# The first phase of an attention and two-layer feed-forward kernel put in order by a list scheduler in the kernel's source

## The chip, the cores and the metric

The kernel runs on one core of one Trainium2 chip. The metric is device time in microseconds (us), lower is better, taken from whole runs; beside them stands one profiled execution, from which every row below comes. The engines are TensorE (PE; its weight loads are listed as PEld), VectorE (DVE), ScalarE (ACT), GpSimd (POOL) and SyncE (SP), which issues the transfers. Each works through its own instructions in the order in which the program lists them.

## What is computed

Causal local attention with a few global keys, then two feed-forward layers:

```python
scores = scale * np.matmul(q, k.transpose(0, 1, 3, 2))      # 4 batches, 8 heads, 768 tokens, 64 wide
keep = is_global | is_local                                  # first 8 keys, or the last 96
scores = np.where(keep, scores + bias, -1e9)                 # bias: minus slope[head] * distance
a = softmax(scores)
x = (a @ v)          # as 3072 tokens x 512
h = x @ w_in         # 512 -> 2048
x = (h - np.tanh(h)) @ w_out
h = x @ w_in2
out = (h * np.cos(h)) @ w_out2
```

The weights of both layers arrive as 8-byte floats.

## The kernel before

**Split numbers.** Each operand of a large product is held as a high part, rounded to the engine's 4-byte format, and a low part, which is the rest. A product is three matmuls: high by high, high by low, low by high. So every value that goes into a matmul costs a copy (high) and a subtraction (low) on some engine.

**Phases.** Phase 0 is the attention and, woven into it, the first half (chunks 0 to 7, of 128 hidden units each) of layer one. Phase 1 is the other half of layer one, phases 2 and 3 are layer two. Only phase 0 is reordered by the change.

**Attention.** A tile i is 128 tokens (24 of them); a quad is a tile and one of two groups g of four heads (48 of them, numbered n = 2i + g). A quad passes these steps: load q and k (`load_qk`); transpose them on PE (`qk_T`, L301 and L303); form high parts on ACT (`qk_hi`, L311, L312) and low parts on DVE (`qk_lo`, L318, L320, L323, L326); scores on PE (`att_s`, L342, 12 matmuls); bias and row minimum on DVE (`att_e`, L362, four a quad); exponent on ACT (L365, four); the sum's reciprocal on DVE (L373, L374) and the four products with it on DVE (`att_n`, L378); transposes on PE (`att_t`, L388, two groups of four, two in the first tile of a batch) copied out by ACT (L390, tile `pt`); and the product with v on PE (`att_v`, L404). After both quads of a tile `att_x` forms the high part of x on ACT (L419) and the low part on DVE (L420), in the tile `xt`.

**Feed-forward of phase 0.** A block j is 256 tokens, which are tiles 2j and 2j + 1; there are 12. For each of its eight chunks f, `ffn_in` runs 12 matmuls (L456), takes tanh on ACT (L464), subtracts on DVE (L465), copies the high part on DVE (L470) and forms the low part on POOL (L471); `ffn_out` runs 12 matmuls (L486) two chunks later. IN(j) below is the first L456 matmul of block j: it needs the low part of tile 2j + 1.

**Weights.** A half is 128 rows or columns of a weight, 512 KB as loaded; phase 0 uses 16. Each passes scale and tail on ACT (L68, L76), join on DVE (L85 and L88), split, which is the high part, on ACT (L97), and the low part on POOL (L98). The 16 halves of phase 1 pass the same steps during phase 0.

**Order.** `in_order` holds each engine to the order in which the source writes phase 0: five `early_quad` calls, then one `quad` call for each further quad, which interleaves attention steps, four `ffn_step` calls (one `ffn_in` or `ffn_out` each) and weight steps (`w_stage`) by hand. `busy` issues matmuls on zeros (L694) where PE would stand idle early on.

Of the kernel before, what the change touches and what calls it, by code (L numbers as in the profile page):

```python
# [102 lines left out]
def attention_ffn_kernel(ctx, tc, q, k, v, n_global, n_local, w1_in, w1_out, w2_in, w2_out, out):  # L103
# [249 lines left out]
    def att_e(i, g, z, pool=None):  # L353

        s, sm, n, m0 = Sb[i, g]
        if pool is None:
            e = pa.tile([128, 2, 256], F32, tag="e", name="e", bufs=3)
        else:
            e = pool.tile([128, 2, 256], F32, tag=("wi", "wo")[z], name="e", bufs=16)
        for j in range(2):  # L360
            col = i * H + 4 * g + 2 * z + j
            nc.vector.tensor_tensor_reduce(  # L362
                out=e[:, j, 0:n], in0=s[j][:, z, 0:n], in1=M[:, z, m0:m0 + n], scale=slopes[4 * g + j] / base,
                scalar=BIG, op0=ALU.add, op1=ALU.min, accum_out=nmall[:, col:col + 1])
            nc.scalar.activation(  # L365
                out=e[:, j, 0:n], in_=e[:, j, 0:n], func=AF.Exp, scale=-1.0,
                bias=nmall[:, col:col + 1], accum_out=sm[:, 2 * z + j:2 * z + j + 1])
        Eb[i, g, z] = e
# [576 lines left out]
```

## Time and profile before

| | us |
|---|---|
| median of three runs (1295.86 to 1297.28) | 1297.21 |
| the profiled execution | 1296.1 |
| its span, first to last instruction | 1294.3 |
| PE, DVE, ACT, POOL busy in the span | 1258.1, 777.7, 571.9, 387.0 |

PE is busy for 97% of the span. A busy share says little by itself where PE waits inside a stretch for other engines: the rows below cut the span where blocks of phase 0 begin. The profiled execution's own time lies 1.1 us under the median of the runs, and 1.8 us over its span.

### The profile page before, as it was taken

The page shows a single profiled execution, that of the slowest core. Times are in us where ns is not written, and L with a number is a line of the kernel's source. Part 1 is how long each engine was busy: PE and PEld are TensorE (multiplying, and loading weights), DVE is VectorE, ACT ScalarE, POOL GpSimd, SP SyncE. Part 2 cuts the span into 40 slices and gives each one's busy share as a digit, 9 for nine tenths or more (in the row PEclk, how much of TensorE's full clock was granted, in tenths as well). Part 3 has the DMA queues.
Part 4 walks back from the last instruction along what each step waited for, and adds up shares of the span by engine and source line. Part 5 has one row for each costly group of instructions (what it writes and reads, how often), then busy time and mean ns, then how long its engine had stood idle before and what let it go on. Part 6 is the DMA issues. An engine that isn't in the chain of part 4 may idle for free.

```text
span 1294.3 us, 20600 instructions
## 1 busy us (share of the span) xinstructions
PE 1258.1 (97%) x7627; PEld 1073.5 (83%) x7630; DVE 777.7 (60%) x1813; ACT 571.9 (44%) x1287; POOL 387.0 (30%) x343
## 2 busy tenths in 40 slices
PE   7779999999999999999999999999999999999997
PEld 4669999999989998888888888888888888888886
DVE  6986677676667642443443456777765565555563
ACT  6865556656556631322332334454444333323331
POOL 1441222222222232544543542333332222222221
PEclk9989999999999999999999999999999999999999
DMA  9424444433343461634554333323220322332110
GB/s 279 139 60 111 113 120 117 125 101 106 97 124 103 111 212 49 211 105 144 197 189 130 131 130 109 122 79 130 82 93 37 130 66 90 106 122 74 65 66 36
DMA packets 160845, 149.28 MB, mean 115 GB/s; under 512 B 84960, under 2 KB 119776, under 8 KB 160736
## 3 DMA queue, kind: packets, MB, share of 16 engines
q1 hardware_dynamic: 160448, 147.88, 36.2%
q8 instruction: 62, 1.02, 0.3%
q14 instruction: 47, 0.39, 0.1%
q10 hardware_dynamic: 288, 0.00, 0.0%
HBM read 103.81 MB, written 44.04 MB: 114 GB/s over the span
## 4 chain that ended last, share of the span: by engine, by line
PE 87%; DVE 6%; ACT 5%; issue 1%; DMA 1%; SPq 0%; DVEq 0%; ACTq 0%
PE h L456 39%; PE o L490 20%; PE o L486 10%; PE c L486 8%; PE x L404 3%; PE s L342 3%; ACT e L365 2%; PE tp L388 2%; DVE wf L85 1%; PE tp L301 1%; DVE e L362 1%; DVE wf L88 1%; DVE e L378 1%; ACT pt L390 1%; PE tp L303 1%
## 5 line engine op out<-in xcount | busy, mean ns | idle before, releaser
L471 POOL TENSOR_TENSOR g<-t,g 128x512 fp32r<-128x512 f32 (+1 forms) x240 | 263.9, 1100 | 767.0 <-DVE g L470 677.8
L456 PE MATMUL h<-x,wi 128*128 128x512 f32 x1728 | 423.4, 394 | 0.0
L456 PEld LDWEIGHTS h<-x,wi 128*128 128x128 f32 x1728 | 324.1, 188 | 75.9
L490 PE MATMUL o<-wo,g 128*128 128x512 f32 x1152 | 275.5, 390 | 0.0
L490 PEld LDWEIGHTS o<-wo,g 128*128 128x128 f32 x1152 | 216.2, 188 | 47.1
L465 DVE TENSOR_TENSOR t<-h,t 128x256 f32<-128x256 f32 (+1 forms) x144 | 73.5, 511 | 212.1 <-ACT t L464 211.9
L456 PE MATMUL h<-xt,wi 128*128 128x256 f32 x1152 | 165.2, 294 | 2.7 <-DVE xt L420 2.6
L486 PE MATMUL c<-g,wo 128*128 128x256 f32 x1152 | 161.4, 290 | 0.0
L456 PEld LDWEIGHTS h<-xt,wi 128*128 128x128 f32 x1152 | 147.2, 195 | 9.0 <-issue 4.1
L464 ACT ACTIVATE t<-h 128x256 f32<-128x256 f32 (+1 forms) x144 | 65.0, 452 | 202.9 <-PE h L456 198.6
L486 PEld LDWEIGHTS c<-g,wo 128*128 128x128 f32 x1152 | 145.0, 192 | 2.1 <-issue 1.9
L441 ACT ACTIVATE t<-t 128x512 f32<-128x512 f32 x96 | 60.8, 633 | 192.4 <-DVE t L440 192.2
L365 ACT ACTIVATE e<-e,nmall 128x256 f32<-128x256 f32 (+1 forms) x192 | 92.8, 485 | 107.5 <-DVE nmall L362 107.5
L486 PE MATMUL o<-g,wo 128*128 128x512 f32 x576 | 139.1, 390 | 0.0
L486 PEld LDWEIGHTS o<-g,wo 128*128 128x128 f32 x576 | 108.1, 188 | 23.8
L443 DVE SCALAR_TENSOR_TENSOR t<-t,h 128x512 f32<-128x512 f32 x96 | 65.9, 686 | 102.0 <-ACT t L442 101.8
L470 DVE CAST g<-t 128x512 fp32r<-128x512 f32 (+1 forms) x240 | 95.2, 397 | 26.4 <-DMA yd<-g 5.2
L438 DVE SCALAR_TENSOR_TENSOR t<-ki,h 128x512 f32<-128x512 int32 x96 | 65.8, 685 | 67.6 <-ACT ki L437 67.2
L437 ACT ACTIVATE ki<-h 128x512 int32<-128x512 f32 x96 | 57.1, 598 | 107.9 <-PE h L456 107.6
L439 DVE SCALAR_TENSOR_TENSOR t<-ki,t 128x512 f32<-128x512 int32 x96 | 87.2, 908 | 2.8
L388 PE MATMUL tp<-ident,e 128*128 128x128 f32 x352 | 57.0, 282 | 15.6 <-ACT pt L390 13.9
L362 DVE CUSTOM_DVE_ANT_0 e<-s,M 128x256 f32<-128x256 f32 (+1 forms) x192 | 68.4, 397 | 4.5 <-PE s L342 3.9
(83 smaller groups left out, 1169.0 us busy)
## 6 DMA issues: line engine op xcount, KB each, us to landing
x<-yd SPq DMA_DIRECT2D x48, 512.0 KB, 5.5
raw<-in_moe_w_in_dram SPq DMA_DIRECT2D x26, 512.0 KB, 3.9
xd<-xt SPq DMA_DIRECT2D x12, 1024.0 KB, 5.4
raw<-in_moe_w_out_dram SPq DMA_DIRECT2D x24, 512.0 KB, 3.5
x<-xd SPq DMA_DIRECT2D x24, 512.0 KB, 6.8
yd<-g SPq DMA_DIRECT2D x24, 512.0 KB, 4.1
qn<-in_q_dram SPq DMA_DIRECT2D x48, 128.0 KB, 2.7
kn<-in_k_dram SPq DMA_DIRECT2D x48, 128.0 KB, 3.2
```

The lines of the kernel that those rows point to most:

```text
L362: nc.vector.tensor_tensor_reduce(out=e[:, j, 0:n], in0=s[j][:, z, 0:n], in1=M[:, z, m0:m0 + n], scale=slopes[4 * g + j] / base, scalar=BIG ...
L365: nc.scalar.activation(out=e[:, j, 0:n], in_=e[:, j, 0:n], func=AF.Exp, scale=-1.0, bias=nmall[:, col:col + 1], accum_out=sm[:, 2 * z + j: ...
L388: nc.tensor.transpose(tp[:, 2 * c + j], e[:, j, c * 128:(c + 1) * 128], ident)
L438: mark[1] = nc.vector.scalar_tensor_tensor(out=r, in0=ki, scalar=-C1, in1=h, op0=ALU.mult, op1=ALU.add)
L439: nc.vector.scalar_tensor_tensor(out=r, in0=ki, scalar=-C2, in1=r, op0=ALU.mult, op1=ALU.add)
L443: nc.vector.scalar_tensor_tensor(out=r, in0=r, scalar=-0.5, in1=h, op0=ALU.add, op1=ALU.mult)
L456: nc.tensor.matmul(h, lhsT=wk[:, a], rhs=x[:, b], start=(n == 0), stop=(n == 3 * KC - 1))
L465: mark[1] = nc.vector.tensor_tensor(out=t, in0=h, in1=t, op=ALU.subtract)
L470: nc.vector.tensor_copy(out=g[:, 0], in_=t)
L471: nc.gpsimd.tensor_tensor(out=g[:, 1], in0=t, in1=g[:, 0].bitcast(F32), op=ALU.subtract)
L486: nc.tensor.matmul(o[z], lhsT=w[:, a, z * 128:(z + 1) * 128], rhs=g[:, b], start=(f == 0 and n == 0 and (P > 0 or z % 2 == 0)), stop=(last ...
L490: nc.tensor.matmul(o[z], lhsT=g[:, a, z * 128:(z + 1) * 128], rhs=w[:, b], start=(f == 0 and n == 0), stop=(last and n == 2))
```

## The change

The hand-written calls of phase 0 are replaced by `Plan`, a list scheduler that runs while the kernel is built. Each step is an `op` with an engine, a cost and a latency in us, a rank, the steps that it needs, and the buffers that it takes and gives back. `solve` repeatedly starts, on the engine that can start first, the op of lowest rank among those that could start within 0.12 us of the earliest; the resulting order is written out and held by `in_order`. `ffn_in` and `ffn_out` are split into their single steps for this, with matmuls in groups of six. The work of phases 1 to 3 is as before.

Beside the order, some steps move between engines in phase 0. The low part of the 16 weight halves of phase 0 goes from POOL to DVE (those of phase 1 stay on POOL). The high part of g goes from DVE (L470) to ACT. In tiles 2 to 7 half of the products with the reciprocal (z = 1) go from DVE to ACT. `fill` puts matmuls on zeros where the plan sees PE idle in its first 100 us: there are 92 of them instead of 45, 22 at the start instead of 5. The last 11 steps of phase 0's feed-forward stay outside the plan. Chunks per block are eight, as before.

```diff
+class Plan:
...
+    def solve(self, near=0.12, look=60, fill=None, switch=0.09):
...
+                first = min(t for t, o in can)
+                t, o = min(((t, o) for t, o in can if t <= first + near), key=lambda c: (c[1]["rank"], c[0]))
+                if best is None or t < best[0]:
+                    best = t, o
...
+    def low(self, w, a, engine):
+        engine.tensor_tensor(out=w[:, 1], in0=a.bitcast(F32), in1=w[:, 0].bitcast(F32), op=ALU.subtract)
...
+    on_act = [(i, 1) for i in range(2, 8)]
...
+            if (i, z) in on_act:
+                nc.scalar.activation(out=e[:, j, 0:n], in_=e[:, j, 0:n], func=AF.Copy, scale=sm[:, c:c + 1])
...
+        if P == 0:
+            nc.scalar.activation(out=g[:, 0], in_=Gt[P, j, f], func=AF.Copy)
+        else:
+            nc.vector.tensor_copy(out=g[:, 0], in_=Gt[P, j, f])
...
+    plan = Plan(s=1, h=2, tp=1, x=1, c0=1, c1=1, e=3, pt=3, q2=2, sm=3, qk=0, v=3, xt=2, g=3, t=3, raw=RAWS, wf=2)
...
+            plan.op(("load",) + key, "SP", 1.6, -11 + 0.6 * m if m < n0 else r - 4, w_load_far if far else w_load,
...
+            plan.op(("low",) + key, *(("DVE", 0.62) if m < n0 else ("POOL", 1.4)), r - 1.4,
+                    lambda key=key, m=m: sp.low(W[key], part.pop(key), nc.vector if m < n0 else nc.gpsimd),
...
+    plan_loads()
+    plan_attention()
+    rest = 11
...
+    plan_weights(plan_ffn(steps), n0, n1)
+    for o in plan.solve(fill=fill):
+        o["run"]()
...
-    for n in range(5):
-        early_quad(n)
-    for n in range(5, len(quads) + 2):
-        if n == 12:
-            flag_n()
-        quad(n)
```

In the changed kernel the lines that answer to those above are: transposes L385 and L387, scores L426, L446 for L362, L454 for L365, products L469 (ACT) and L471 (DVE), transposes of e L481, copy L487, v L501, x L513 and L518, IN L561, tanh L570, subtraction L575, high part of g L583 (ACT), low part of g L590, OUT L615, join L156 and L159, weight low part L171, zeros L825.

**SP, the first transfers.** q and k of tile 0 come first (four rows), then, before the change:

```order
L283 DMA qn_121<-in_q_dram 128x4x64
L283 DMA kn_123<-in_k_dram 128x4x64
L290 DMA vn_125<-in_v_dram 128x8x64
L59 DMA raw_127<-in_moe_w_in_dram 128x4x256
L283 DMA qn_129<-in_q_dram 128x4x64
L283 DMA kn_131<-in_k_dram 128x4x64
```

and after it:

```order
L374 DMA vn_144<-in_v_dram 128x8x64
L130 DMA raw_146<-in_moe_w_in_dram 128x4x256
L130 DMA raw_148<-in_moe_w_in_dram 128x4x256
L367 DMA qn_197<-in_q_dram 128x4x64
L367 DMA kn_199<-in_k_dram 128x4x64
L130 DMA raww_201<-in_moe_w_in_dram 128x4x256
L374 DMA vn_208<-in_v_dram 128x8x64
L130 DMA raww_229<-in_moe_w_out_dram 128x1024
L367 DMA qn_257<-in_q_dram 128x4x64
L367 DMA kn_259<-in_k_dram 128x4x64
```

The last pair in each is q and k of tile 1, second group: three more weight halves and one more v stand ahead of it than before; 12 further halves follow it before anything else.

**DVE, the work around the low part of x of tile 1** (xt), before the change:

```order
L378 TENSOR_SCALAR e<-e,sm 128x256 x4
L85 SCALAR_TENSOR_TENSOR wf<-raww 128x512
L88 SCALAR_TENSOR_TENSOR wf<-raww,wf 128x512
L318 SCALAR_TENSOR_TENSOR q_548<-tp,qs,q_548 128x256
L320 TENSOR_TENSOR kw_96<-tp,kw_96 128x2x128
L326 CAST kw_96<-kg_98 128x4x32
L373 TENSOR_SCALAR sm<-sm 128x4
L374 RECIPROCAL sm<-sm 128x4
L378 TENSOR_SCALAR e<-e,sm 128x256 x4
L420 TENSOR_TENSOR xt<-x,xt 128x4x128
```

and after it:

```order
L471 TENSOR_SCALAR e<-e,sm 128x256 x4
L171 TENSOR_TENSOR wi<-wf,wi 128x512 x2
L156 SCALAR_TENSOR_TENSOR wf<-raww 128x512
L159 SCALAR_TENSOR_TENSOR wf<-raww,wf 128x512
L156 SCALAR_TENSOR_TENSOR wf<-raww 128x512
L159 SCALAR_TENSOR_TENSOR wf<-raww,wf 128x512
L171 TENSOR_TENSOR wo<-wf,wo 128x512
L156 SCALAR_TENSOR_TENSOR wf<-raww 128x512
L159 SCALAR_TENSOR_TENSOR wf<-raww,wf 128x512
L171 TENSOR_TENSOR wi<-wf,wi 128x512
L518 TENSOR_TENSOR xt<-x,xt 128x4x128
```

Joins and the new low parts of weights (L171) now fill DVE here, and the attention of later quads has moved behind.

**PE, where a later block begins** (the last row is its IN), before the change:

```order
L342 MATMUL s<-kw_97,q_4883 128x256 x12
L404 MATMUL x<-pt,vn 64x128 x8
L486 MATMUL c_4686<-g,wo 128x256 x6
L486 MATMUL c_4687<-g,wo 128x256 x6
L388 MATMUL tp<-ident,e 128x128 x2
L456 MATMUL h<-xt,wi 128x256 x12
```

and after it:

```order
L615 MATMUL c_4724<-g,wo 128x256 x6
L481 MATMUL tp<-ident,e 128x128 x2
L615 MATMUL c_4725<-g,wo 128x256 x6
L426 MATMUL s<-kw_97,q_4974 128x256 x12
L501 MATMUL x<-pt,vn 64x128 x8
L481 MATMUL tp<-ident,e 128x128 x2
L426 MATMUL s<-kw_96,q_5106 128x256 x12
L561 MATMUL h<-xt,wi 128x256 x24
```

The x row is the product with v that completes the block's input. Between it and IN stood 12 OUT matmuls and two transposes; now two (elsewhere four) transposes and the 12 score matmuls of the next quad, and all OUT matmuls of the old block come earlier.

## Rows read from the trace of the kernel before

**Rows 1.** Windows; columns: stretch, length, busy PE, PEld, DVE, ACT, POOL, clock, DMA share, GB/s.

```profile
0.00:40.90 40.90, 32.71 (x218) 19.89 (x221) 29.50 (x116) 27.84 (x80) 7.11 (x18) 1.00 1.01 283
40.90:94.70 53.80, 41.22 (x341) 38.05 (x341) 48.46 (x111) 38.61 (x94) 23.43 (x20) 0.90 0.26 72
94.70:135.60 40.90, 38.23 (x352) 36.07 (x351) 25.54 (x95) 20.89 (x60) 6.56 (x9) 0.96 0.35 95
135.60:465.70 330.10, 325.46 (x3061) 306.45 (x3060) 225.01 (x786) 198.75 (x566) 74.45 (x89) 1.00 0.40 110
```

**Rows 2.** Timeline of PE: start, length, instruction, idle time before; blocks 0 to 2 begin.

```profile
1.20 2.31 PE L694 MATMUL idle<-zero 128*128 128x512 bf16 x5 [1.20 <-DVE zero L699]
...
40.91 0.38 PE L456 MATMUL h<-xt,wi 128*128 128x256 f32 x1
...
94.66 0.36 PE L456 MATMUL h<-xt,wi 128*128 128x256 f32 x1
...
135.61 1.68 PE L456 MATMUL h<-xt,wi 128*128 128x256 f32 x12
```

**Rows 3.** Waits, 41 to 135 us: total, times, longest.

```profile
PE tp L388 <- ACT pt L390: 11.3, 5, 4.8
```

**Rows 4.** Lines, 41 to 94.7 us, of DVE and POOL: busy, mean ns, idle before.

```profile
L88 DVE SCALAR_TENSOR_TENSOR wf<-raww,wf 128x512 int32<-128x512 int32 x12 | 11.6, 970 | 0.4
L85 DVE SCALAR_TENSOR_TENSOR wf<-raww 128x512 int32<-128x512 int32 x12 | 10.8, 901 | 0.0
L378 DVE TENSOR_SCALAR e<-e,sm 128x256 f32<-128x256 f32 x16 | 7.4, 520 | 0.1
...
L98 POOL TENSOR_TENSOR wo<-wf,wo 128x512 fp32r<-128x512 f32 x7 | 9.8, 1401 | 5.4 <-ACT wo L97 5.4
L98 POOL TENSOR_TENSOR wi<-wf,wi 128x512 fp32r<-128x512 f32 x5 | 8.2, 1642 | 2.6 <-ACT wi L97 2.6
L471 POOL TENSOR_TENSOR g<-t,g 128x256 fp32r<-128x256 f32 x8 | 6.3, 784 | 23.2 <-DVE g L470 17.6 <-DVE sm L373 5.7
```

**Rows 5.** Timeline of DVE early on, and 60 us later beside POOL.

```profile
19.82 0.69 DVE L85 SCALAR_TENSOR_TENSOR wf<-raw 128x512 int32<-128x512 int32 x1
...
21.22 0.48 DVE L318 SCALAR_TENSOR_TENSOR q<-tp,qs,q 128x256 fp32r<-128x256 f32 x1
...
21.96 0.41 DVE L362 CUSTOM_DVE_ANT_0 e<-s,M 128x256 f32<-128x256 f32 x1
...
22.30 0.42 DVE L362 CUSTOM_DVE_ANT_0 e<-s,M 128x256 f32<-128x256 f32 x1
...
28.66 1.14 DVE L378 TENSOR_SCALAR e<-e,sm 128x256 f32<-128x256 f32 x4
...
32.20 0.69 DVE L420 TENSOR_TENSOR xt<-x,xt 128x512 fp32r<-128x512 f32 x1
...
62.09 1.84 POOL L98 TENSOR_TENSOR wi<-wf,wi 128x512 fp32r<-128x512 f32 x1 [0.85 <-ACT wi L97]
...
62.81 1.67 DVE L88 SCALAR_TENSOR_TENSOR wf<-raww,wf 128x512 int32<-128x512 int32 x1
```

**Rows 6.** DMA view, 0 to 41 us.

```profile
DMA packets 18292, 11.59 MB, mean 283 GB/s; under 512 B 13168, under 2 KB 17264, under 8 KB 18288
```

**Rows 7.** DMA issues of the whole span: KB each, median us to landing.

```profile
qn<-in_q_dram SPq DMA_DIRECT2D x48, 128.0 KB, 2.7
```

**Rows 8.** Timeline of all engines where block 5 begins.

```profile
243.43 0.98 PE L342 MATMUL s<-kw,q 64*128 64x256 f32 x12
...
244.34 1.09 PE L404 MATMUL x<-pt,vn 128*64 128x128 f32 x16
...
245.48 0.60 ACT L419 ACTIVATE xt<-x 128x512 fp32r<-128x512 f32 x1 [2.10 <-PE x L404]
246.11 0.69 DVE L420 TENSOR_TENSOR xt<-x,xt 128x512 fp32r<-128x512 f32 x1 [2.40 <-ACT xt L419]
...
247.04 0.36 PE L456 MATMUL h<-xt,wi 128*128 128x256 f32 x1
```

More of the change, by code (lines that the diff above doesn't have):

```diff
@@ L27 @@
 RAWS = 2
+RAMP = 16
 @contextmanager
@@ L351, in attention_ffn_kernel, with att_r @@
     Eb = {}
-    def att_e(i, g, z, pool=None):
+    def att_r(i, g, z, j, pool=None):
         s, sm, n, m0 = Sb[i, g]
[L356 to L368, printed above, removed]
@@ L478, in ffn_out @@
+        ffn_cast(P, j, f)
+        ffn_low(P, j, f)
+    def ffn_out(P, j, f, zs=range(4)):
+        w, g = W[P // 2, f, "wo"], G[P, j, f]
+        first, last = (f == chunks(P, j)[z] for z in (0, -1))
+        if first and P == 0 and zs[0] == 0:
             c = [ps_c.tile([128, 2, N1], F32, tag=f"c{z}", name=f"c{z}", bufs=1) for z in range(2)]
             acc[P, j] = [c[z // 2][:, z % 2] for z in range(KC)] + c
-        elif f == 0:
+        elif first and P > 0:
             acc[P, j] = [late["ps_o"][z // 2].tile([128, 512], F32, tag=f"o{z}", name=f"o{z}", bufs=1) for z in range(4)]
@@ L482, in ffn_out @@
         o = acc[P, j]
-        for z in range(4):
+        for z in zs:
             for n, (a, b) in enumerate(((0, 0), (0, 1), (1, 0))):
@@ L809, in attention_ffn_kernel @@
-    seq = [None]
+            nc.tensor.matmul(t, lhsT=zero[:, 0:128], rhs=zero[:, 0:t.shape[1]], start=True, stop=True)
+    seq = []
+    nout = [0] * 4
     for P in range(4):
-        steps = [(P, j, f) for j in range(NB[P]) for f in range(NH)]
+        steps = [(P, j, f) for j in range(NB[P]) for f in chunks(P, j)]
+        nout[P] = len(steps)
         done = 0
@@ L816, in attention_ffn_kernel @@
             due = []
-            while done < len(steps) and (
-                    done <= n - LAG[P] or (P > 0 and done == n - LAG[P] + 1 and steps[done][2] == NH - 1)):
+            while done < len(steps) and (done <= n - LAG[P] or (
+                    P > 0 and done == n - LAG[P] + 1 and steps[done][2] == chunks(*steps[done][:2])[-1])):
                 due.append(("out",) + steps[done])
@@ new lines, in attention_ffn_kernel, with fill, run @@
+    part = {}
+    out_started = [False]
+    def fill(plan, order, t0, t1):
+        if t0 > 100 or t1 < t0 + 0.4:
+            return
+        if plan.tiles["c1"] and not any(o["key"][0] == "out" for o in order):
+            run = lambda: busy(idle, int((t1 - t0 - 0.1) / 0.23))
+        else:
+            into = next((o for o in plan.ops if o["key"][0] == "in" and o["start"] is None), None)
+            if not into or into["key"][3] or (into["take"] and (
+                    plan.key["s", 1, 1]["start"] is None or not plan.tiles["h"] or min(plan.tiles["h"]) > t0)):
+                return
+            if into["take"]:
+                into["take"] = ()
+                plan.tiles["h"].remove(min(plan.tiles["h"]))
+            def run():
+                if not hz:
+                    hz.append(h_tile(0, into["key"][2]))
+                busy(hz[0], int((t1 - t0 - 0.1) / 0.12))
+        order.append(dict(key=("busy",), start=t0 + 0.01, run=run))
@@ L884, in attention_ffn_kernel @@
+    plan_loads()
+    plan_attention()
+    rest = 11
+    steps = []
+    while seq[-rest - 1][1] == 0:
+        steps.append(seq.pop())
+    ndone[0] = len([x for x in steps if x[0] == "out"])
+    n0, n1 = 2 * len(chunks(0, NB1 - 1)), 2 * len(chunks(0, NB1 - 1)) + 2 * len(chunks(1, 1))
+    plan_weights(plan_ffn(steps), n0, n1)
+    for o in plan.solve(fill=fill):
+        o["run"]()
+    for _ in range(RAWS):
+        w_load()
+    late[0, "stages"] = 4 * (n1 - n0)
+    planned[0] = False
     strict[0] = False
```

523 lines of the change are left out of this document (323 added, 200 removed).

## The prediction

> **What bounds the kernel now.** The reader starts with the windows [rows 1], cut where blocks of phase 0 begin [rows 2]. From 135.6 to 465.7 us PE is busy 325.46 of 330.10 us: nine blocks at 36.7 us each with 4.6 us of idle in all. No order of the same matmuls can take more than that from this stretch. After 493.5 us the program lists the same work as before. So the place to win is the first 135.6 us. There PE is busy for 112.2 us, part of it on zeros, and each stretch has another limit.
>
> In the first (IN(0) at 40.9) the 16 DMA engines are busy throughout (share 1.01, 283 GB/s) and DVE works 29.5 us. In the second (IN(0) to IN(1), 53.8 us against 36.7 in the steady stretch) DVE is busy 48.5 us: it is the bound. PE's largest wait there is for `pt`, the copy on ACT, 11.3 us in five waits [rows 3] (ACT works 38.6 us). The lines of DVE in that stretch show a second loss [rows 4]: a join half that takes 0.69 us by itself [rows 5] has a mean of 0.90 (L85) and 0.97 (L88) us there, and a product with the reciprocal 0.52 us. The timeline shows why: the L88 at 62.81 us takes 1.67 us and ends as POOL's weight subtraction does, which began at 62.09 and took 1.84 [rows 5]. In the third (IN(1) to IN(2), 40.9 us) PE is nearly the bound again: 38.2 us busy, at a granted clock of 0.96 of the full 2.4 GHz on the mean.
>
> **The change, part by part.** Sums are made on the profiled execution (1296.1 us) and carried over to the median of the runs (1297.21), 1.1 above it.
>
> *Up to IN(0).* DVE's count up to the low part of x of tile 1, before and after: q and k low pairs 7 and 4, row minima 20 and 16, products 20 and 16, joins 4 and 6, weight low parts 0 and 5. Prices from start to start [rows 5]: a join 1.40 us (19.82 to 21.22), a q and k pair 0.74, a row minimum 0.34, a product (1.14 - 0.09) / 4 = 0.26. For the weight's low part on DVE there is no row; nearest is the subtraction L420 over as many elements, 0.69 us long, 0.60 occupied if it overlaps its neighbour by 0.09 as those do. It can hardly be under two products (0.52, half the elements each) nor over POOL's mean of 1.40 to 1.64 us [rows 4]; I take 0.60. The sum: -2.2 - 1.4 - 1.0 + 2.8 + 3.0 = +1.2, and about -1.0 for the narrow ones that go with two quads fewer. So DVE has the same 29.5 us before IN(0), of which 11.4 more were idle before. What its idle time will be is set by the loads. Ahead of and with the last q and k pair of tile 1 the queue held 1.84 MB and now holds 3.67 MB (halves of 512 KB, q and k 128 KB each, v 256 KB); at 283 GB/s [rows 6] that is 6.5 and 13.0 us. Add the first issue at about 0.8 us and 2.7 us to landing [rows 7]: 16.5 us, say 17, at best. Behind that pair's DVE work stand, in order, twelve products (four of them of 128 elements, priced alike), eight row minima, four joins, five low parts and two x subtractions: 3.1 + 2.7 + 5.6 + 3.0 + 1.2 = 15.6 us and about 1 us of narrow ones. With the pair itself 0.74, its transposes and ACT copies about 1.1 and four exponents that DVE waits for about 1.5 us, the low part of x is done at 17 + 16.6 + 3.3 = 36.9, and IN(0), with the transposes of tile 2 just ahead of it on PE, starts at 38. The 22 zero matmuls at the start, at 0.46 us (five in 2.31 us [rows 2]), last up to 10.2 us, to 11.4; the pair at 17 hides them, except that two quads' scores start later than they could. Range 35 to 41.
>
> *IN(0) to IN(1).* DVE's counts between the low parts of x of tiles 1 and 3: q and k pairs 4 and 7 (+2.2), row minima 16 and 24 (+2.7), products 16 and 12, ten others being on ACT (-1.0), joins 13 and 10 (-4.2), weight low parts 0 and 11 (+6.6), casts of g 8 and 0 (-2.1, priced as a product), narrow ones and one more y copy (+2.0, an estimate): +6.2 us. Against it stands what POOL took from DVE: 12 x 0.28 + 12 x 0.21 + 16 x (0.52 - 0.35) = 8.6 us. POOL was busy there for 24.3 us, 18.0 of them on the 12 weight subtractions that leave it; in proportion 6.4 us come back. DVE would be busy 48.5 + 6.2 - 6.4 = 48.3 us. Its idle time was 5.3. ACT, at 38.6, gains 18 copies or products of 256 elements and loses 12 weight steps of 512; from the 0.60 us copy of 512 [rows 8], at 0.3 to 0.6 us for 256, that and the eight more exponents make 41 to 49 us. Two engines this full, each in a fixed order, will wait for each other; I take 3.2 us of DVE idle: 51.5 us, range 48.5 to 54. IN(1): 89.5, 5.2 us earlier.
>
> The Trainium skill (SBUF — State Buffer, SBUF: two separate sides) says that the port pair shared by VectorE and GpSimd is an exclusive lock, held for a whole instruction, and that a VectorE instruction with two SBUF inputs takes it against a GpSimd one that reads SBUF. The 1.67 us L88 agrees. By the page up to the whole 18.0 us of POOL's weight work might come back, and IN(1) would stand 11 us lower still; the rows of means show 8.6 us lost to all 24.3 us of POOL, and the measurement decides.
>
> *IN(1) to IN(2).* The same PE work before and after (96 IN, 96 OUT, four quads' scores). 40.9 us less the 2.7 us idle is 38.2 with the clock as it was; I take 38, range 36.7 to 41. IN(2): 127.5, 8.1 us earlier. And the order has done more before it: 12 OUT matmuls, one quad's 12 score matmuls and two transposes, 1.5 + 0.9 + 0.2 = 2.6 us of PE (12 matmuls of a chunk: 1.68 us long [rows 2], some 0.15 of it beside the next). Lead: 10.7 us.
>
> *The steady stretch.* The counts per block are equal. What is new is how a block begins. Before, from the end of the product with v (245.43) it took ACT's copy, DVE's subtraction and signals 1.6 us to IN (247.04) [rows 8], and 12 OUT matmuls (1.5 us) and two transposes filled them. Now two or four transposes and the score matmuls do (0.2 to 0.45 and 0.98 us): 0.2 to 0.4 us short at each of nine blocks, and up to 0.6 us more where ACT is within another instruction. That is 2 to 9 us, less what a better order saves of the 4.6 us; I take a loss of 2.5, range -4.6 to +9.
>
> The sum: -10.7 + 2.5 = -8.2. The profiled execution would read 1287.9, the runs **1289.0 us**.
>
> **The rivals.**
>
> *Everything meshes (1280).* DVE at 48.3 with hardly any idle, IN(0) at 36, blocks 0 and 1 in 49 and 36.7: IN(2) at 121.7, 13.9 earlier, and 2.6, and no loss later: 16.5. For it: the order is made by readiness, and POOL no longer slows the joins. Against it: ACT and DVE are both near full.
>
> *The ramp stays as it was (1295).* IN(0) at 40.9, since loads and 22 zero matmuls push the first scores; block 0 at 53.5, since low parts (6.6 us) eat what POOL gave back (6.4); block 1 at 38: -3.2 - 2.6 + 3.5 = -2.3. For it: the two terms are nearly equal, and their idle time is my choice.
>
> *Slower (1304).* The fixed order has little slack where a block begins: IN waits for x, and the copy on ACT can stand behind exponents that wait for DVE. Price: 2 us of PE at each of nine blocks is 18, less 10.7: +7.3. It decides from 10.7 / 9 = 1.2 us per block, and from 1.5 the loss can be told. For it: the chain of 1.6 us with nothing spare, and the low part of the last g, which its OUT now needs only 24 matmuls and four transposes after its IN. Against it: 4.6 us of idle in 330 show how well PE is fed by two to three chunks of lag, which are kept.
>
> **How the numbers follow.** Forecast 0.51, meshing 0.17, unchanged ramp 0.17, slower 0.15. A measurement of this kernel tells about 0.2% (2.6 us) from no change. The forecast, with its ends, is faster in 0.47 and the same in 0.04; the unchanged ramp splits 0.06 and 0.10 with 0.01 slower; so faster 0.70, same 0.14, slower 0.16. For 8 in 10 the range runs from 1279, where meshing lies, to 1302, where two thirds of the slower case are left out.
>
> **What would show it.** Right: IN(0) near 38, IN(1) near 89.5, IN(2) near 127.5; the mean of L159 (L88 before) near 0.7 us in the first 90 us and POOL without weight subtractions there; the low part L171 at 0.69 us; PE idle 5 to 10 us between IN(2) and IN(11), most of it ahead of the first L561 of a block, put down to L518. Wrong: IN(0) past 41 (loads or zero matmuls), DVE's idle time in block 0 over 6 us with ACT as releaser (the moved copies), or block lengths beyond 38 us in the steady stretch.

## The result, and the profile after

The changed kernel takes 1282.97 us (median of four runs, 1282.77 to 1284.22), beside 1297.22 of the kernel before: a ratio of 0.9895, with a 95% interval of 0.9877 to 0.9912. That is 14.2 us less; 8.2 were forecast. The span of the profiled execution falls from 1294.3 to 1281.1 us, by 13.2, which is what the stretches below add up to.

The windows of the changed kernel, cut as in [rows 1] at IN(0), IN(1), IN(2), IN(11) and the end of phase 0 (columns: stretch, length, busy PE, PEld, DVE, ACT, POOL, clock, DMA share, GB/s):

```profile
0.00:38.84 38.84, 34.98 (x231) 19.52 (x234) 29.48 (x103) 30.52 (x80) 1.94 (x14) 1.00 0.98 288
38.84:89.63 50.79, 45.01 (x406) 40.12 (x404) 46.90 (x138) 43.88 (x123) 6.70 (x8) 0.97 0.34 91
89.63:126.28 36.65, 36.65 (x351) 34.51 (x349) 19.75 (x71) 26.43 (x78) 7.60 (x9) 1.00 0.45 125
126.28:453.60 327.32, 324.57 (x3047) 304.54 (x3045) 203.94 (x703) 217.09 (x631) 74.11 (x88) 1.00 0.37 104
453.60:480.97 27.37, 27.03 (x208) 26.17 (x209) 5.70 (x11) 9.57 (x22) 7.29 (x9) 1.00 0.76 260
```

Cut at the same places, the kernel before has 40.91, 53.75, 40.95, 330.13 and 27.71 us:

| stretch | before | forecast | after | gain |
|---|---|---|---|---|
| up to IN(0) | 40.91 | 38 | 38.84 | 2.1 |
| block 0, IN(0) to IN(1) | 53.75 | 51.5 | 50.79 | 3.0 |
| block 1, IN(1) to IN(2) | 40.95 | 38 | 36.65 | 4.3 |
| IN(2) to IN(11) | 330.13 | 330.0 | 327.32 | 2.8 |
| IN(11) to the end of phase 0 | 27.71 | same | 27.37 | 0.3 |
| the rest of the span | 800.9 | same | 800.1 | 0.7 |

(The forecast for the fourth stretch is 2.5 us of new idle time less the 2.6 us of work done ahead.) Each stretch gave something, and the largest single gap to the forecast is the fourth, where a loss was expected.

In block 0 the groups of DVE, and POOL's only group, answer to [rows 4] (busy, mean ns, idle before):

```profile
L156 DVE SCALAR_TENSOR_TENSOR wf<-raww 128x512 int32<-128x512 int32 x10 | 7.4, 740 | 0.0
L159 DVE SCALAR_TENSOR_TENSOR wf<-raww,wf 128x512 int32<-128x512 int32 x10 | 7.3, 735 | 0.3
L171 DVE TENSOR_TENSOR wo<-wf,wo 128x512 fp32r<-128x512 f32 x7 | 4.7, 685 | 0.0
L471 DVE TENSOR_SCALAR e<-e,sm 128x256 f32<-128x256 f32 x12 | 4.5, 414 | 0.2
...
L590 POOL TENSOR_TENSOR g<-t,g 128x256 fp32r<-128x256 f32 x8 | 6.7, 837 | 74.8 <-ACT g L583 74.8
```

The join halves are back to 0.74 us from 0.90 and 0.97, the products to 0.41 from 0.52, and the low part of a weight takes 0.685 us on DVE, the length that was assumed for it.

### The profile page after: what moved, and what is told of

It is laid out like the page before. It is cut to its first block, busy times and chain, and to the rows that moved or that the text cites. A ratio compares the mean times of both kernels' runs of the same rounds, so it can differ in the third digit from the quotient of the medians.

```text
span 1281.1 us, 20646 instructions
## 1 busy us (share of the span) xinstructions
PE 1260.5 (98%) x7674; PEld 1070.4 (84%) x7677; DVE 750.2 (59%) x1709; ACT 607.5 (47%) x1407; POOL 366.3 (29%) x327
## 4 chain that ended last, share of the span: by engine, by line
PE 89%; ACT 5%; DVE 4%; issue 1%; DVEq 0%; ACTq 0%
PE h L561 39%; PE o L619 20%; PE o L615 10%; PE c L615 9%; PE tp L481 3%; PE x L501 3%; PE s L426 2%; ACT e L454 2%; PE idle L825 1%; DVE e L471 1%; DVE e L446 1%; PE tp L385 1%; PE tp L387 1%; DVE wf L156 1%; DVE q L402 0%
## 5 line engine op out<-in xcount | busy, mean ns | idle before, releaser
L590 POOL TENSOR_TENSOR g<-t,g 128x512 fp32r<-128x512 f32 (+1 forms) x240 | 266.6, 1112 | 817.4 <-DVE g L585 455.1
L561 PE MATMUL h<-x,wi 128*128 128x512 f32 x1728 | 423.8, 394 | 0.0
L561 PEld LDWEIGHTS h<-x,wi 128*128 128x128 f32 x1728 | 324.0, 188 | 75.8
L575 DVE TENSOR_TENSOR t<-h,t 128x256 f32<-128x256 f32 (+1 forms) x144 | 73.4, 511 | 179.1 <-ACT t L570 178.7
L561 PE MATMUL h<-xt,wi 128*128 128x256 f32 x1152 | 160.8, 289 | 1.0 <-ACT xt L513 0.7
L615 PE MATMUL c<-g,wo 128*128 128x256 f32 x1152 | 160.6, 286 | 0.0
L570 ACT ACTIVATE t<-h 128x256 f32<-128x256 f32 (+1 forms) x144 | 65.0, 454 | 198.0 <-PE h L561 188.7
L561 PEld LDWEIGHTS h<-xt,wi 128*128 128x128 f32 x1152 | 143.7, 190 | 4.9 <-issue 1.0
L615 PEld LDWEIGHTS c<-g,wo 128*128 128x128 f32 x1152 | 146.3, 191 | 0.3
L615 PE MATMUL o<-g,wo 128*128 128x512 f32 x576 | 139.1, 390 | 0.0
L615 PEld LDWEIGHTS o<-g,wo 128*128 128x128 f32 x576 | 108.1, 188 | 23.7
L454 ACT ACTIVATE e<-e,nmall 128x256 f32<-128x256 f32 (+1 forms) x192 | 92.4, 486 | 37.8 <-DVE nmall L446 37.8
L446 DVE CUSTOM_DVE_ANT_0 e<-s,M 128x256 f32<-128x256 f32 (+1 forms) x192 | 66.3, 398 | 31.7 <-PE s L426 30.9
L585 DVE CAST g<-t 128x512 fp32r<-128x512 f32 x144 | 67.8, 472 | 23.4 <-DMA yd<-g 12.0
L481 PE MATMUL tp<-ident,e 128*128 128x128 f32 x352 | 57.1, 281 | 7.7 <-ACT pt L487 3.3
```

Source lines behind the costliest of these rows:

```text
L446: nc.vector.tensor_tensor_reduce(out=Eb[i, g, z][:, j, 0:n], in0=s[j][:, z, 0:n], in1=M[:, z, m0:m0 + n], scale=slopes[4 * g + j] / base, ...
L454: nc.scalar.activation(out=e[:, j, 0:n], in_=e[:, j, 0:n], func=AF.Exp, scale=-1.0, bias=nmall[:, col:col + 1], accum_out=sm[:, 2 * z + j: ...
L481: nc.tensor.transpose(tp[:, 2 * c + j], e[:, j, c * 128:(c + 1) * 128], ident)
L561: nc.tensor.matmul(h, lhsT=wk[:, a], rhs=x[:, b], start=(kc == 0 and n == 0), stop=(kc == KC - 1 and n == 2))
L575: mark[1] = nc.vector.tensor_tensor(out=t, in0=Hb.pop((P, j, f)), in1=t, op=ALU.subtract)
L585: nc.vector.tensor_copy(out=g[:, 0], in_=Gt[P, j, f])
```

## The experiments

The runs of before made beside the experiments had medians of 1296.4 to 1297.0 us. Stretches are those of the table above, in us; "run" is the median, the ratio is to the runs of before beside it.

| kernel | IN(0) | block 0 | block 1 | at half | IN(2) to IN(11) | run | ratio (95%) |
|---|---|---|---|---|---|---|---|
| before | 40.91 | 53.75 | 40.95 | 13.7 | 330.13 | 1297.2 | 1 |
| after | 38.84 | 50.79 | 36.65 | 3.4 | 327.32 | 1283.0 | 0.9895 (0.9877 to 0.9912) |
| before, low parts on DVE | 44.09 | 54.33 | 40.55 | 13.7 | 330.10 | 1299.9 | 1.0024 (1.0014 to 1.0033) |
| after, low parts on POOL | 37.82 | 51.95 | 36.41 | 0 | 327.38 | 1283.9 | 0.9901 (0.9886 to 0.9916) |
| scheduler alone | 38.38 | 56.36 | 36.62 | 6.8 | 326.25 | 1287.2 | 0.9924 (0.9911 to 0.9938) |
| after, high part of g on DVE | 38.71 | 51.11 | 36.88 | 0 | 325.99 | 1282.3 | 0.9892 (0.9877 to 0.9908) |
| after, products on DVE | 38.66 | 51.92 | 38.12 | 6.8 | 327.74 | 1286.3 | 0.9921 (0.9907 to 0.9934) |
| after, no planned zeros | 39.62 | 52.59 | 36.98 | 6.8 | 327.39 | 1286.0 | 0.9917 (0.9904 to 0.9931) |
| after, 5 zeros at the start | 38.48 | 50.90 | 36.65 | 3.4 | 327.39 | 1283.6 | 0.9899 (0.9883 to 0.9916) |
| after, scores behind IN | 38.50 | 50.63 | 36.64 | 3.4 | 330.89 | 1286.8 | 0.9927 (0.9914 to 0.9941) |
| after, q and k of tile 1 first | 38.59 | 48.74 | 37.73 | 0 | 327.24 | 1281.75 | 0.9887 (0.9872 to 0.9902) |
| the same, high part of g on DVE | 38.22 | 52.64 | 36.91 | 0 | 326.02 | 1283.9 | 0.9901 (0.9885 to 0.9918) |
| and ScalarE's measured costs | 47.24 | 42.75 | 36.84 | 0 | 325.90 | 1283.0 | 0.9894 (0.9878 to 0.9911) |
| q and k first, 5 zeros | 38.52 | 48.79 | 37.74 | 0 | 327.35 | 1281.9 | 0.9891 (0.9874 to 0.9907) |

The column "at half" gives the time between IN(0) and IN(2) in which the granted clock was at its lower level, 1.2 GHz. In the changed kernel this is one stretch, from 74.0 to 77.4 us, with PE busy for 3.35 of its 3.42 us; at full level the same work would take up to 1.7 us less:

```profile
73.97:77.39 3.42, 3.35 (x24) 2.69 (x26) 3.35 (x14) 3.42 (x14) 0.47 (x1) 0.50 0.34 76
```

The edits below move this column too. So where two planned kernels differ in it, a difference of a few us between them is not the edited step's alone, and no run here separates the two.

**1. The low parts of the weights alone, in the hand-written order.**

```diff
-            W[key] = sp.split(key, key[2])
+            W[key] = sp.split(key, key[2], nc.vector if nsplit[0] < 2 * NH else None)
```

> The kernel before, in its hand-written order, with one part of the change: the low parts of the 16 weight halves of phase 0 on VectorE, right behind the split. Theory A (in the hand-written order a step put on VectorE costs what it takes, since VectorE is the bound of block 0 there): 12 low parts at 0.60 to 0.69 us between IN(0) and IN(1) are 7.2 to 8.3 us more, against 6.4 to 8.6 us that the joins and products get back when GpSimd no longer works beside them; block 0 stays within 1.5 us of its 53.8, IN(0) within 1.5 us of 40.9, and the whole is 1294 to 1300. Rival B (GpSimd beside VectorE was the cost, and the move by itself brings the gain): joins at 0.70 to 0.74 us on the mean instead of 0.90 to 0.97, block 0 in 51 or less, the whole 1291 to 1294. Against both stands a third: the low part now stands on VectorE right behind a split that ScalarE has not done, so VectorE waits there for ScalarE; then block 0 is 55 to 60 and the whole 1299 to 1304.

It is slower by 3.1 us. Theory A had the size of the whole, at its upper edge, but not the place. The third case had the size too (1299 to 1304) and the wait for the split on ACT, but put block 0 at 55 us or more. Nearly all is lost ahead of IN(0): DVE's busy time there rises by 1.4 us, with four low parts of 0.69 us each in it, and its idle time by 1.8, the size of one wait for a split (1.9). The windows of this kernel up to IN(1), DVE's waits for splits, up to IN(0) and then in block 0, and PE's largest wait in block 0, of this kernel and then of the kernel before (total, times, longest):

```profile
0.00:44.09 44.09, 34.35 (x219) 21.06 (x222) 30.89 (x120) 28.29 (x80) 1.93 (x14) 0.96 0.92 262
44.09:98.42 54.33, 41.63 (x340) 38.11 (x341) 45.12 (x122) 39.01 (x94) 6.36 (x8) 0.91 0.26 71
```

```profile
DVE wo L98 <- ACT wo L97: 1.9, 1, 1.9
```

```profile
DVE wo L98 <- ACT wo L97: 2.7, 2, 1.3
...
DVE wi L98 <- ACT wi L97: 1.3, 1, 1.3
```

```profile
PE tp L388 <- ACT pt L390: 10.1, 4, 4.7
```

```profile
PE tp L388 <- ACT pt L390: 10.9, 4, 4.8
```

Up to IN(1) DVE has 16 low parts (11 us) more than before and is busy for 76.0 us instead of 77.9, so POOL's absence does give time back: the join halves of block 0 are at 0.73 and 0.69 us, about as rival B had them. In block 0 DVE is busy for 45.1 us, 3.3 less than before; yet the block is 0.6 us longer. DVE now waits 4.0 us there for splits on ACT, which takes up what was freed, and PE's wait for `pt` is nearly what it was. So in the hand-written order the move buys nothing, because the low part stands right behind its split. Whether DVE's work sets block 0 in that order is not told by this run.

**2. The low parts back on POOL, in the planned order.**

```diff
-            plan.op(("low",) + key, *(("DVE", 0.62) if m < n0 else ("POOL", 1.4)), r - 1.4,
-                    lambda key=key, m=m: sp.low(W[key], part.pop(key), nc.vector if m < n0 else nc.gpsimd),
+            plan.op(("low",) + key, "POOL", 1.4, r - 1.4,
+                    lambda key=key, m=m: sp.low(W[key], part.pop(key), nc.gpsimd),
```

> The changed kernel with the low parts of the 16 halves of phase 0 back on GpSimd, planned again at 1.4 us each. Theory A (the order carries the gain of the ramp; the move of the low parts is nearly even, for it gives VectorE as much work as it takes away in slower joins): IN(0) within 1.5 us of 38.8, block 0 within 1.5 us of 50.8, the whole 1281.5 to 1285. Rival B (the move carries it): joins at 0.85 to 0.97 us on the mean in block 0, block 0 back at 53 to 55, the whole 1286 to 1290.

Theory A holds for the whole: 1283.9 against 1283.0, no difference that can be told, and IN(2) is at 126.18 against 126.28. Rival B is right that the joins slow down (0.96 and 1.03 us, above its 0.85 to 0.97), and wrong on the time. Their groups in block 0 of this kernel, and POOL's:

```profile
L159 DVE SCALAR_TENSOR_TENSOR wf<-raww,wf 128x512 int32<-128x512 int32 x10 | 10.3, 1032 | 0.3
...
L156 DVE SCALAR_TENSOR_TENSOR wf<-raww 128x512 int32<-128x512 int32 x9 | 8.6, 955 | 0.6 <-POOL wo L171 0.6
L471 DVE TENSOR_SCALAR e<-e,sm 128x256 f32<-128x256 f32 x10 | 5.3, 574 | 0.2
...
L171 POOL TENSOR_TENSOR wo<-wf,wo 128x512 fp32r<-128x512 f32 x7 | 10.0, 1425 | 8.8 <-ACT wo L167 8.8
...
L171 POOL TENSOR_TENSOR wi<-wf,wi 128x512 fp32r<-128x512 f32 x4 | 5.2, 1298 | 2.6 <-ACT wi L167 2.6
```

Eleven low parts leave DVE, 7.4 us by the rows of after. The joins and products then take 10 x 0.30 + 9 x 0.22 + 10 x 0.16 = 6.6 us more, and DVE's busy time is 46.2 instead of 46.9 us. The move is an even exchange, as the prediction's two terms (6.6 against 6.4 us) had it. The Trainium skill (SBUF — State Buffer, SBUF: two separate sides) has the port pair that VectorE and GpSimd share as a lock held for the whole instruction. The trace agrees with the sign: here 6.6 of POOL's 15.2 us of such work show in DVE, less than half of what the lock could cost at most.

**3. The scheduler alone** (low parts on POOL, high part of g and all products on DVE, planned again).

> The list scheduler alone: the changed kernel with the low parts of the weights on GpSimd, the high part of g on VectorE and all products with the reciprocal on VectorE, as before, planned again. Theory A (the order carries most of the 14.2 us): the whole 1283 to 1287, block 1 still near 36.7 and the nine blocks behind it at 327 to 328. Rival B (the moved steps carry it): block 0 has 4 us more on VectorE (8 high parts at 0.21, 10 products at 0.26) and slower joins, so 54 to 57; the whole 1288 to 1294. The stretch from IN(2) to IN(11) tells by itself whether its 2 us less idle time of TensorE come from the order (327 to 328) or from the high part of g on ScalarE (329.5 to 331).

The whole is 1287.2: 9.5 of some 14 us come from the scheduler, with the matmuls on zeros that it plans. Experiment 5 prices those zeros at 3 us in the changed kernel; no run has the order without them and without the moved steps. The windows of blocks 0 and 1 and of the stretch behind them:

```profile
38.38:94.74 56.36, 46.78 (x409) 42.20 (x407) 51.95 (x141) 38.59 (x105) 21.64 (x19) 0.94 0.34 88
94.74:131.36 36.62, 36.62 (x351) 34.53 (x349) 26.43 (x91) 22.57 (x67) 8.56 (x10) 1.00 0.42 118
131.36:457.61 326.25, 323.18 (x3048) 304.18 (x3046) 237.79 (x781) 190.85 (x550) 72.01 (x87) 1.00 0.38 104
```

Block 1 is as short as in the changed kernel and the stretch behind it shorter: both are the scheduler's. Block 0 is longer than before, with 52 us of DVE work in it. Theory A is right on block 1, and its 327 to 328 us for the stretch behind were too many; rival B is right on block 0. The whole lies between their ranges, 0.2 us above that of A.

**4. The high part of g, and the products, back on DVE, one at a time.**

```diff
-            nc.scalar.activation(out=g[:, 0], in_=Gt[P, j, f], func=AF.Copy)
+            nc.vector.tensor_copy(out=g[:, 0], in_=Gt[P, j, f])
...
-                plan.op(("cast", j, f), "ACT", 0.31, r, lambda j=j, f=f: ffn_cast(0, j, f),
+                plan.op(("cast", j, f), "DVE", 0.21, r, lambda j=j, f=f: ffn_cast(0, j, f),
```

> The changed kernel with the high part of g back on VectorE (planned there at 0.21 us), the low parts of the weights and half of the products staying where the change put them. With the list scheduler alone, block 0 took 56.4 us and the whole 1287.2, with the low parts on GpSimd but the other two moves made 51.95 and 1283.9. Theory A (VectorE is the bound of block 0 under the planned order: block 0 is its busy time and 4 to 4.5 us): 8 high parts, 0.21 to 0.3 us each, put 1.7 to 2.4 us on VectorE between IN(0) and IN(1); block 0 52.5 to 53.2, the whole 1284.5 to 1286, and the nine blocks from IN(2) to IN(11) stay within 1 us of 327.3. Rival B (ScalarE, 43.9 us busy in block 0, limits it as much; giving it 8 copies less pays for what VectorE takes on): block 0 within 0.7 us of 50.8, the whole 1282 to 1284.

```diff
-    on_act = [(i, 1) for i in range(2, 8)]
+    on_act = []
```

> The changed kernel with all products with the reciprocal on VectorE, as before, the other two moves staying. Theory A (VectorE is the bound of block 0 under the planned order): ten products at 0.26 us put 2.6 us on VectorE between IN(0) and IN(1), and four or so more before IN(0) 0.5 to 1 us; block 0 53 to 54, the whole 1285 to 1287; together with the run that puts the high part of g back it should account for the 4 us by which the list scheduler alone stayed behind. Rival B (ScalarE limits block 0 as much; the ten products there, at 0.40 us from start to start, are 4 us that it gets back): block 0 within 0.7 us of 50.8, the whole 1282 to 1284.

Without the move of g the run is 1282.3, so the move shows no worth, and rival B has the numbers. Its reason is not shown. The window of block 0 of this kernel has TensorE at full level throughout, and DVE's busy time there is no longer than in the changed kernel (46.65 against 46.90 us), for its joins and products come out shorter by about as much as the eight copies take:

```profile
38.71:89.82 51.11, 45.63 (x414) 39.79 (x413) 46.65 (x146) 41.16 (x115) 7.50 (x8) 1.00 0.33 90
```

The move of the products is worth 3.3 us: theory A is right on the whole (1286.3), though not on the place, since block 0 is only 1.1 us longer and block 1 another 1.5. The two edits together should have made up the 4.2 us by which the scheduler alone stays behind; they give -0.7 and +3.3. Fewer matmuls are done ahead of IN(1) without the products' move (387 matmul records of the trace against 406 in block 0, 368 against 351 in block 1), as the windows show:

```profile
38.66:90.58 51.92, 44.28 (x387) 39.18 (x386) 47.63 (x139) 37.62 (x106) 6.62 (x8) 0.93 0.30 81
90.58:128.70 38.12, 38.12 (x368) 35.69 (x366) 25.02 (x88) 26.31 (x78) 8.86 (x10) 1.00 0.47 131
```

Set against DVE's busy time from IN(0) to IN(2), the four planned kernels form a row: 66.7 us of it (after) go with IN(2) at 126.3, 70.0 (g back) with 126.7, 72.7 (products back) with 128.7 and 78.4 (scheduler alone) with 131.4. So a later IN(2) goes with more work on DVE, by some 0.4 us for each. That is not the price of a microsecond on DVE by itself, since TensorE is at half level for 3.4, 0, 6.8 and 6.8 us in these four.

**5. No zeros but the first five.**

```diff
-    for o in plan.solve(fill=fill):
+    for o in plan.solve():
```

> The changed kernel without the matmuls on zeros that the plan fills in; only the five at the start stay, as before had them at that place. Theory A (the zeros keep TensorE at its full level: with 92 of them the granted clock was at half for one stretch of 3.4 us after 5.7 us, with 45 before it was at half up to 16.9 us and in four stretches between 57 and 103 us): the granted clock stays at half well into the first 40 us and drops again in block 0; IN(0) 40 to 43, IN(1) 92 to 96, the whole 1285 to 1291. Rival B (VectorE sets IN(0) and block 0; TensorE at half level has room there): IN(0) within 1 us of 38.8, the whole 1281 to 1284. A gain is possible too: the 22 zeros at the start end at 8.3 us and hold back the first transposes, which stood at 4.0 to 7.4 before; that would bring IN(0) to 37 and the whole to 1280 to 1282.

Theory A: 3 us slower, though IN(0) is a little earlier than its 40 to 43. The granted clock reaches its full level only at 39.2 us (5.7 in the changed kernel) and is at half again from 73.3 to 80.1 us, twice as long as the changed kernel's one stretch (74.0 to 77.4). IN(0) comes 0.8 us later, block 0 takes 1.8 us more. (The trace records the clock only from its first rise on, and ahead of that the clock column reads 1.00, here and in [rows 1].)

```profile
0.00:39.62 39.62, 28.44 (x150) 18.02 (x150) 28.22 (x101) 30.21 (x78) 1.94 (x14) 1.00 0.92 275
39.62:92.21 52.59, 45.72 (x401) 40.34 (x401) 48.16 (x140) 44.92 (x124) 7.27 (x8) 0.94 0.35 91
```

The timeline of PE in this kernel shows the level by itself: two transposes take 0.69 us at 38.0 and 0.38 at 39.3.

```profile
38.04 0.69 PE L385 MATMUL tp<-ident,qn 128*128 128x128 f32 x2
...
39.28 0.38 PE L387 MATMUL tp<-ident,kn 128*128 128x128 f32 x2
```

Without the zeros PE's order is the same but for them (7585 matmul records in the same sequence); so the level of the clock is worth these 3 us, although PE has idle time there.

**6. Five zeros at the start instead of 22.**

```diff
-        if t0 > 100 or t1 < t0 + 0.4:
+        if t0 > 100 or t0 < 1 or t1 < t0 + 0.4:
```

> The changed kernel with 5 matmuls on zeros at the start instead of 22; the plan's later ones (from its first 1 us on) stay. In the changed kernel the 22 run from 1.2 to 8.3 us, the granted clock is at full level from 5.7 us on, and the first transposes of q and k start at 8.17; in the kernel before, with 5, they ran from 4.0 to 7.4 us, and the clock was at half up to 16.9. Theory A (the 22 hold back the first q and k pair, and with it all of VectorE's work up to IN(0), which runs without a gap from 16 us on): first low parts of q and k on VectorE at 7 to 8.5 us instead of 9.65, IN(0) at 37 to 38.2, the whole 1281 to 1282.5. Rival B (what the pair gains is lost on transposes and scores at half level, 0.66 instead of 0.38 us for two transposes, and the other idle time of VectorE ahead of 16 us, for the bias and tile 1, stays): IN(0) 38.4 to 39.5, the whole 1282.5 to 1284.5.

DVE's first low parts come at 7.65 us instead of 9.65, as theory A had it, and IN(0) only 0.4 us earlier (38.48); that and the run, 1283.6, are within rival B's ranges. Of the 2 us, 1.5 are lost again on two of DVE's waits for ACT (0.9 us for a weight half, 0.6 more for exponents).

**7. The scores behind IN, in blocks 3 to 10.**

```diff
-                    need=[("ql", i, g)] + [("s",) + p for p in prev], take=[(bank, banks), ("sm", 1)],
+                    need=[("ql", i, g)] + [("s",) + p for p in prev] + ([("in", (n - 3) // 4, 0, 0)] if n >= 18 and n % 4 == 2 else []),
+                    take=[(bank, banks), ("sm", 1)],
```

> The changed kernel with one rule more in the plan: in blocks 3 to 10 the scores of the next quad come behind the first IN matmul of the block instead of ahead of it, so that between the product with v that completes x and IN only four (or two) transposes are left to cover the copy on ScalarE and the subtraction on VectorE. Theory A (from the end of that product to IN are 1.45 us in the changed kernel, of which 0.6 us of transposes and 0.95 of scores cover all; the steady stretch lost nothing because this cover just suffices): without the scores TensorE stands idle for 0.8 to 1.2 us at each of eight blocks, its idle time between IN(2) and IN(11) goes from 2.75 to 9 to 12 us, released by the subtraction of x, and the whole is 1289 to 1292.5. Rival B (TensorE makes the time up inside the block, or the blocks are held by something else): idle there rises by under 2 us and the whole is 1282 to 1285.

It costs 3.6 us between IN(2) and IN(11) and 3.8 in the run: the mechanism of theory A at half its size or less, 0.45 us per block. PE's idle time there is 5.6 us instead of 2.75, and the run lies between the two ranges. The timeline of all engines where block 5 begins, first of the changed kernel, then of this one, shows why (start, length, instruction):

```profile
233.95 1.09 PE L501 MATMUL x<-pt,vn 128*64 128x128 f32 x16
...
234.98 0.44 PE L481 MATMUL tp<-ident,e 128*128 128x128 f32 x2
...
235.19 0.58 ACT L513 ACTIVATE xt<-x 128x512 fp32r<-128x512 f32 x1
...
235.35 0.98 PE L426 MATMUL s<-kw,q 64*128 64x256 f32 x12
...
235.79 0.69 DVE L518 TENSOR_TENSOR xt<-x,xt 128x512 fp32r<-128x512 f32 x1 [0.79 <-ACT xt L513]
...
236.25 1.51 PE L561 MATMUL h<-xt,wi 128*128 128x256 f32 x9
```

```profile
235.37 0.57 ACT L513 ACTIVATE xt<-x 128x512 fp32r<-128x512 f32 x1
...
235.97 0.69 DVE L518 TENSOR_TENSOR xt<-x,xt 128x512 fp32r<-128x512 f32 x1 [0.79 <-ACT xt L513]
...
236.00 0.39 PE L561 MATMUL h<-xt,wi 128*128 128x256 f32 x1 [0.39 <-ACT xt L513]
...
236.72 1.47 PE L561 MATMUL h<-xt,wi 128*128 128x256 f32 x10 [0.34 <-DVE xt L518]
```

The first IN matmul reads the high part of x alone and starts as soon as ACT's copy ends (235.94), while DVE is still at the low part; only the second waits for that. So IN(j) does not need the low part of x, as was said of it ahead of the prediction; the matmul behind it does. From the end of the product with v (235.24) it is 0.76 us to the first and 1.48 to the second. In the changed kernel the first starts 1.21 us after the product (235.04) because PE has transposes and scores until then, and PE does not wait at all.

**8. q and k of tile 1 loaded first.**

```diff
-                    plan.op(("qk", i, g), "SP", 0.8, -12 + n if i == 1 else n - 3.3, lambda i=i, g=g: load_qk(i, g),
+                    plan.op(("qk", i, g), "SP", 0.8, -18 + n if i == 1 else n - 3.3, lambda i=i, g=g: load_qk(i, g),
```

> The changed kernel with q and k of tile 1 loaded ahead of the first weight halves and of v (the last pair of tile 1 was issued at 11.2 us, behind 3.7 MB, and transposed at 17.0 us; now it is issued at about 5 us), planned again. Theory A (the landing of that pair sets IN(0): from its transposes on VectorE works nearly without a gap up to the low part of x of tile 1): the pair is transposed by 13 us, IN(0) comes at 35.5 to 37.5, the whole is 1279.5 to 1282. Rival B (VectorE has the same sum of work ahead of IN(0) and its idle time lies before 10 us, where the first pair and the bias keep it waiting; and the weight halves land 0.5 MB later, 1.8 us at 283 GB/s): IN(0) within 1 us of 38.8, and block 0 the same or up to 1 us longer, the whole 1282 to 1285.

Rival B holds for IN(0): the last pair of tile 1 lands at 9.1 us instead of 17.2, is transposed at 17.2 all the same, and IN(0) moves by 0.25 us. What shortens is block 0, by 2.05 us, of which block 1 gives 1.1 back (16 matmul records move into it). It need not be the earlier loads by themselves: TensorE is at full level throughout this block 0, and the 3.4 us at half level in the changed kernel can account for up to 1.7 us. The whole, 1281.75, is that of theory A: 1.2 us less than the changed kernel, within what a measurement can tell. The window of its block 0:

```profile
38.59:87.33 48.74, 44.93 (x399) 38.73 (x398) 45.48 (x135) 43.03 (x120) 6.54 (x8) 1.00 0.33 88
```

**9. Three combinations.**

> A version meant to beat both kernels, made of the two edits that lost nothing: the high part of g back on VectorE (by itself 1282.3, the stretch from IN(2) to IN(11) 326.0 instead of 327.3 us), and q and k of tile 1 loaded first (by itself 1281.75, block 0 48.7 us instead of 50.8). Theory A (the two gains lie in different stretches and add up): IN(2) at 125 to 126, IN(2) to IN(11) 326 us, the whole 1280 to 1281.5. Rival B (in block 0 the copies of g take VectorE's time back that the earlier loads had given, since with the first edit alone block 0 was 51.1): block 0 50 to 51.5, the whole 1281.5 to 1283.

> The version with both edits (high part of g on VectorE, q and k of tile 1 first), with the plan's costs of ScalarE's steps as the trace of the changed kernel shows them from start to start: exponent 0.495 instead of 0.45 us, scale and tail 0.565 instead of 0.515, split 0.52 instead of 0.48, copy of transposes 0.48 instead of 0.45. The computation is the same; only the order moves. Theory A (the plan believes ScalarE some 9% faster than it is, so engines wait for it in block 0, where VectorE has 3.9 us of idle time): block 0 1 to 2 us shorter than without the new costs, the whole 1278.5 to 1280.5. Rival B (the order is greedy, and a new cost gives another order, no better one: the sums of VectorE, not its waits, set the block): within 1.5 us of the version without them, to either side, 1280 to 1283.

> A version meant to beat both kernels: q and k of tile 1 loaded first (by itself 1281.75 us, IN(2) at 125.06) and 5 matmuls on zeros at the start instead of 22 (by itself 1283.6, IN(2) at 126.03 instead of 126.28, first low parts of q and k at 7.65 us instead of 9.65). Theory A (with the loads of tile 1 early, the 2 us by which VectorE starts sooner are no longer lost waiting for that tile): IN(0) at 37 to 38, IN(2) at 123.5 to 124.7, the whole 1280 to 1281.3. Rival B (in either kernel VectorE finds the same other waits ahead of IN(0), on ScalarE's exponents and on the weight halves, which the loads set): IN(0) within 0.5 us of 38.6, IN(2) 124.7 to 125.5, the whole 1281.3 to 1282.5.

None adds up. With g's high part on DVE as well, block 0 goes back to 52.6 us (somewhat beyond rival B's ranges, as the run of 1283.9 is). With ScalarE's costs set right the plan starts IN(0) 9 us later and has done so much ahead by then that IN(1) comes 0.9 us earlier than without them: 1283.0, rival B. With five zeros added to the early loads nothing changes (1281.9, rival B). The two kernels with early loads are the fastest, 1281.75 and 1281.9: below both kernels, though against the changed one by no more than a measurement can tell.

## Why the prediction was right, and where it was not

The sign and the range held; the gain was under-forecast by 6 us. By its own steps:

**Up to IN(0)** (38, measured 38.84). The count of DVE's work (29.5 us) came out at 29.48, and the pair's landing, put at 17 us, at 17.2, though by other terms: 5.6 us from issue to landing, where 2.7 had been taken, and an earlier issue. Of the joins five, not four, lie behind the pair, which is 1.4 us, more than the miss. But the argument that the landing sets IN(0) fell: experiment 8 took 8 us off it and moved IN(0) by 0.25. The number came out because the planned order transposes the pair at 17 us anyway, which was luck as far as the landing goes; from 16.3 us on DVE stands idle for only 1.3 us before IN(0). The 22 zeros at the start were priced at half level throughout and put at up to 11.4 us; the clock rose at 5.7 and they ended at 8.3.

**IN(0) to IN(1)** (51.5, measured 50.8). Three parts of this step came out: DVE at 48.3 us busy (46.9), ACT at 41 to 49 (43.9), 3.2 us of DVE idle time (3.9). The step's premise that DVE was the bound before stays open: experiment 1 freed 3.3 us of DVE and the block grew, but 4.0 us of new waits stood in their place. In the planned order less work on DVE goes with a shorter ramp (experiment 4), with the clock's level beside it. Two readings of this step were off. Of the 11.3 us that PE waits for `pt` [rows 3], 10.9 are in block 0. And the L88 at 62.81 us does not end with POOL's subtraction: by [rows 5] that ends at 63.93 and L88 at 64.48, 0.55 us later, which is most of a join half and fits a wait for the subtraction with the join behind it.

**IN(1) to IN(2)** (38, measured 36.65). This term was mis-sized: it removed the 2.7 us of idle time and kept the clock. The block is now 36.65 us with PE busy throughout at full level. Before, the clock was 0.96 there [rows 1], which is 1.6 us of 40.9, and 40.95 - 2.7 - 1.6 = 36.65.

**The steady stretch** (a loss of 2.5, measured a gain of 2.8). This step failed. The 1.6 us that [rows 8] show between the product with v and IN were read as the time that x needs; they were the time that PE had other work. Experiment 7 shows what x needs, 0.76 us to the first matmul and 1.48 to the second, and that with only four or two transposes in between a block loses 0.45 us. With the scores there is no wait for x at all. PE's waits between IN(2) and IN(11), of the changed kernel and then of the kernel before (total, times, longest):

```profile
PE tp L481 <- DVE kw L404: 1.4, 8, 0.2
PE tp L481 <- DVE kw L410: 0.7, 2, 0.4
```

```profile
PE tp L301 <- ACT pt L390: 2.7, 9, 0.5
PE tp L388 <- ACT pt L390: 1.8, 2, 1.0
```

PE's idle time fell from 4.6 to 2.75 us. So 1.9 us of idle time were saved where a loss of 2.5 was forecast. The other 0.9 of the 2.8 us is less busy time of PE: of the work ahead at IN(2), the 12 score matmuls and two transposes (put at 1.1 us) are paid back in this stretch, while the 12 OUT matmuls (1.5 us) are still ahead at IN(11).

**The rivals.** Block 1 and the steady stretch went as in the meshing case, IN(0) and block 0 as in the forecast, and 1283 lies between their 1289 and 1280. The unchanged ramp was right on the low parts (an even exchange, experiment 2) and left out that the scheduler with its zeros, and the products, shorten the ramp all the same. The slower case had its mechanism in experiment 7, where it costs 0.45 us per block, far from the 1.2 from which it would decide.

**What stays open.** Why the stretch from IN(2) to IN(11) is 1.3 us shorter with the high part of g on DVE (326.0 against 327.3) is not settled: PE has as many matmuls there and is busy for 322.95 instead of 324.57 us. What sets block 0, in either order, is not settled either, nor how much of the scheduler's 9.5 us its zeros bring, nor what single edits would give at one and the same level of the clock. No run put back the order of one stretch alone.

## What to carry to other kernels

The start of an instruction says when its engine came to it, not when its input was ready: to price a wait, look for a place where the engine was idle before it, or make one. An engine with the largest busy time of a stretch need not be its bound. Test that by taking work off it, and look at what stands in the place of that work: in the hand-written order 4.0 us of new waits took up the 3.3 us that had been freed. When two kernels are compared, compare the granted clock of their stretches too, since an edit on another engine can move it. Gains of single edits do not add up under a greedy scheduler, since each edit makes another order; measure the combination.

## What the runs showed of the hardware

A subtraction of two 128x512 operands in SBUF takes 0.685 us on VectorE and 1.3 to 1.4 on GpSimd, and the latter lengthens VectorE's joins beside it from 0.74 to 0.96 and 1.03 us, so that giving it to GpSimd frees almost nothing. The granted clock had an effect in a stretch where TensorE seemed to have room: at half level up to 39.2 us and for 6.8 us in block 0, it cost 3 us.
